# Reordering the first block of a fused SSM and GEGLU kernel: contraction outermost over seven PSUM banks, weights loaded by rows

## The chip, the cores and the metric

The kernel runs on one core of a Trainium2 chip. The metric is the device time of one execution in microseconds (us). Before the change it is 178.35 us, the median of 4 runs (178.12 to 178.73). A profile of one execution shows where the time goes; its engines are PE (TensorE, matrix products), PEld (its weight loads), DVE (VectorE), ACT (ScalarE), POOL (GpSimd) and SP (SyncE, which here only issues DMAs).

## The reference

The input x has 2048 rows (tokens) of 512 values. Everything runs on its normalized form, and three terms are added up:

```python
def _layernorm(x, axis=-1, eps=1e-5):
    m = jnp.mean(x, axis=axis, keepdims=True)
    v = jnp.var(x, axis=axis, keepdims=True)
    return (x - m) / jnp.sqrt(v + eps)

# A: a diagonal state space model, D = P = 512
    dt = jnp.exp(log_dt); Lam_bar = jnp.exp(dt * Lam)
    B_bar = ((Lam_bar - 1.0) / Lam)[:, None] * Bmat
    Bu = jnp.einsum("bld,pd->blp", x + 0j, B_bar)
    for t in range(L):
        h = Lam_bar[None, :] * h + Bu[:, t, :]
    y = 2.0 * jnp.einsum("blp,dp->bld", hseq, Cmat).real + x * Dskip[None, None, :]

# B: a gated feed-forward layer, F = 1376
    return (_gelu(x @ w_gate) * (x @ w_up)) @ w_down

    xn = _layernorm(x, axis=-1)
    return x + _A_ref(xn, ...) + _B_ref(xn, ...)
```

All inputs are bf16, and so is the output.

## The kernel before, in words

The tokens are cut into four blocks of 512 and each block into four tiles of 128. Per block the kernel normalizes (`LN`), turns the normalized tiles so that the 512 features lie on the partitions (`TR`, a transposing DMA into `XNT`), multiplies by B (`BU`), runs the scan on VectorE in a rotated frame (`CHAIN`), multiplies by w_gate and w_up and joins the two with GELU (`GU`), and sums states and hidden values into the output (`DN`). The program order of TensorE is the order of the calls at the end of `build`: the first stretch described below, `GU(0, [7, 8, 9, 10])`, `BU(0)`, `BU(1)`, `GU(1)`, `BU(2)`, `DN(0)` and so on to `DN(3)`.

Three things set the order of the rest. Operations on TensorE and DMAs on SP's queue run in the order in which they are written. Those of the other engines, DMAs on ACT's queue among them, are ordered by a planner (`Sched`): it works back from due times with assumed durations and assigns each engine its list. `order_behind` ties an operation behind another one. Semaphore waits follow from the buffers that operations read and write.

Block 0 has no weights and no x at its start, and is treated on its own. The first 896 of the 1376 columns of w_gate and w_up (seven of eleven column tiles) are computed with the tokens as rows (L684 to L711); `GU(0)` does the other four column tiles as in all later blocks. In the first stretch

- SP loads x tile by tile, w_gate and w_up in chunks of columns (`FCH`: 384, 256, 256 and the last 480), all 512 rows of a chunk at once (L505 to L514, `load_W` at L536). ACT's queue loads x's tile 1, half of the first gate chunk and the three small parameter vectors (`load_par`, L516), which a transposing DMA turns (`tr_par`, L521).
- TensorE warms up on seven 512-column products of a tile of zeros (`fwarm`, L914; `fill`, L921, repeats such products 128 columns wide).
- VectorE takes mean and variance of a tile (`stats`, L624 and L625), subtracts the mean (`sub`, L933, L941), and TensorE turns the centred tile in four 128-column transposes (`cent_T`, L673), which ACT copies from PSUM to `XC` (L680).
- `GT_mm` (L698) multiplies a centred tile by a range of columns (`FR`) of gate and up, with all four contraction steps k in succession in one PSUM bank. `GT_evac` takes GELU with the row's 1/sigma as scale on ACT (L707) and multiplies by up and 1/sigma on VectorE (L710, "hmul") into `H0`, which a DMA turns later (`H0_T`).
- POOL takes the square root of the variances (L631) after VectorE's L630; L636 is the reciprocal and L643 the full normalization, whose result `TR(0)` (L722) turns for `GU(0)` and `BU(0)`.

The order of calls in that stretch is: transposes of tiles 0 and 1; gate products of both for the first 384 columns; up products; then whole units (tile, column range), all four k at once, tiles 2 and 3 centred and turned in between.

`params` and `tables_dve` compute the scan's coefficients on POOL and VectorE from the turned parameters.

Of the kernel before, what the change touches and what calls it, by code (L numbers as in the profile page):

```python
# [77 lines left out]
class Sched:  # L78
# [95 lines left out]
    def _backward(self, span):  # L174
# [11 lines left out]
        while n:  # L186
# [26 lines left out]
            for d in op.deps:  # L213
                late[d.id] = min(late[d.id], begin[op.id] - LAT(d, op))
                left[d.id] -= 1
                if left[d.id] == 0 and d.eng not in INORDER:
                    ready[d.eng].append(d)
        return begin

    def _forward(self, prio):  # L220
# [13 lines left out]
        def rdy_time(op):  # L234
            return max([d.finish + LAT(d, op) for d in op.deps] + [op.nb])
# [55 lines left out]
    def emit(self):  # L291
# [19 lines left out]
        for e in ENGINES:  # L311
            seen = {}
            prog = []
            for op in order[e]:
                need = {}
                for d in op.deps:
                    if d.kind == "eng" and d.eng == e and (e == "tensor" or d is op.behind):
                        continue
                    key = ("e", d.eng) if d.kind == "eng" else ("d", d.id)
                    if seen.get(key, 0) >= d.val:  # L320
                        continue
                    if key not in need or need[key].val < d.val:
                        need[key] = d
# [49 lines left out]
def build(nc, ins, out):  # L373
    with ExitStack() as es:
# [16 lines left out]
        FCH = [(0, 384), (384, 640), (640, 896), (896, F)]  # L391
        WGc = [Buf("WGc%d" % i, "sbx", 10 * i, 10 * i + 1) for i in range(4)]
        WUc = [Buf("WUc%d" % i, "sbx", 100 + 10 * i, 101 + 10 * i) for i in range(4)]
# [65 lines left out]
        XCs = [[Buf("XC%d_%d" % (j, n), "xc", 2 * j + n, 2 * j + n + 1) for n in range(2)] for j in range(4)]  # L459
        H0_all = A.alloc("H0", [4, 896], BF16, at=SSb[2].lo); H0 = ring(H0_all, "H0_", 4)  # L460
        IOTJ = A.alloc("IOTJ", [512], I32, at=OUTB_all.lo)
        A1 = A.alloc("AA", [KP, 512], F32, at=TA.lo)
# [29 lines left out]
        def ld_w(W, Wc, src, ci, queue="sync", after=()):  # L492
            f0, f1 = FCH[ci]
            return S.dma(lambda e: e.dma_start(W.ap[:, :, f0:f1], src[:, f0:f1].rearrange("(k p) f -> p k f", p=128)),
                         512 * (f1 - f0) * 2, writes=[Wc[ci]], tag="ld_w", queue=queue, after=after)
# [3 lines left out]
        WG0h = [Buf("WG0h%d" % n, "sbx", n / 2, (n + 1) / 2) for n in range(2)]  # L499

        def ld_wg0(n, queue, after=()):
            return S.dma(lambda e: e.dma_start(WG.ap[:, 2 * n:2 * n + 2, 0:384],
                                        ins["B_w_gate"][256 * n:256 * (n + 1), 0:384].rearrange("(k p) f -> p k f", p=128)),
                  192 * 1024, writes=[WG0h[n]], tag="ld_w", queue=queue, after=after)
        ld_x0(0)  # L505
        S.order_behind(ld_x0(1, "scalar", [wrm]), GATE["table"])
        ld_wg0(0, "sync")
        S.order_behind(ld_wg0(1, "scalar", [wrm]), GATE["table"])
        ld_x0(2)
        ld_w(WU, WUc, ins["B_w_up"], 0)  # L510
        ld_x0(3)
        for ci in (1, 2):
            ld_w(WG, WGc, ins["B_w_gate"], ci)
            ld_w(WU, WUc, ins["B_w_up"], ci)  # L514

        def load_par():  # L516
            for q, nm in enumerate(("A_log_dt", "A_Lambda_re", "A_Lambda_im")):
                S.dma(lambda e, q=q, nm=nm: e.dma_start(PROW.ap[4 * q:4 * q + 4, :], ins[nm].rearrange("(s p) -> s p", p=128)),
                      1024, writes=[PROWq[q]], tag="ld_" + nm, queue="scalar", after=[half])

        def tr_par():  # L521
            S.dma(lambda e: e.dma_start_transpose(PAR.ap.rearrange("p q t -> p (q t)").unsqueeze(1), PROW16.ap), 4096,
                  reads=PROWq, writes=[PAR], tag="tr_par", issue=900.0)
# [12 lines left out]
        def load_W():  # L536
            ld_w(WG, WGc, ins["B_w_gate"], 3)
            ld_w(WU, WUc, ins["B_w_up"], 3)

# [8 lines left out]

        wchunk = lambda ft: 0 if ft < 3 else (1 if ft < 5 else (2 if ft < 7 else 3))
# [113 lines left out]
        def cent_T(j, banks, engs="A"):  # L663
            per = KD // len(engs)
            for n, eng in enumerate(engs):
                bank = banks[n]
                pt = PS[bank].bitcast(BF16)

                def f(e, n=n, pt=pt):
                    ins_ = None  # L670
                    for q in range(per):
                        k = per * n + q
                        ins_ = e.transpose(pt[:, 128 * q:128 * (q + 1)], XN[j].ap[:, 128 * k:128 * (k + 1)], IDN.ap)  # L673
                    return ins_
                PE(f, 56.0 * per, [XN[j], IDN], [BANK[bank]], "T0")
                dst = XC_all.ap[:, per * n:per * (n + 1), 128 * j:128 * (j + 1)]
                src = pt[:, 0:128 * per].rearrange("p (q t) -> p q t", q=per)
                w = [XCs[j][n]] if len(engs) == 2 else XCs[j]
                if eng == "A":
                    GATE["evTA"] = ACT(lambda e, src=src, dst=dst: e.activation(dst, src, ACTF.Copy), d_act(128 * per), [BANK[bank]], w, "evT")  # L680
                else:
                    V(lambda e, src=src, dst=dst: e.tensor_copy(dst, src), 110 + 0.6 * 128 * per, [BANK[bank]], w, "evT")

        FR = ((0, 192), (192, 384), (384, 640), (640, 896))  # L684

        def GT_mm(j, r, bank, us, ks=range(KD)):
            f0, f1 = FR[r]
            w = f1 - f0
            ci = max(0, r - 1)
            Wc = [(WGc, WUc)[u][ci] for u in us]  # L690
            if ci == 0 and us == [0] and len(ks) == 2:
                Wc = [WG0h[ks[0] // 2]]
            dst = PS[bank][:, w * us[0]:w * (us[-1] + 1)].rearrange("p (w f) -> p w f", w=len(us))

            def f(e):
                ins_ = None
                for k in ks:
                    ins_ = e.matmul(dst, XCd(j, k), WGU[:, us[0]:us[-1] + 1, k, f0:f1], start=(k == 0), stop=(k == KD - 1))  # L698
                return ins_
            PE(f, d_pe([w * len(us)] * len(ks)), Wc + XCs[j][ks[0] // 2:ks[-1] // 2 + 1], [BANK[bank]], "GT")  # L700

        def GT_evac(j, r, bank, rs):
            f0, f1 = FR[r]
            w = f1 - f0
            GATE["nh"] = kk = (GATE["nh"] + 1) % 3
            sc, rb = rs
            GATE["last_gelu"] = ACT(lambda e: e.activation(GG[kk].ap[:, 0:w], PS[bank][:, 0:w], ACTF.Gelu_apprx_tanh, scale=sc),  # L707
                                    d_act(w, 1), [BANK[bank], rb], [GG[kk]], "gelu")
            hp = Buf("H0_%d_%d" % (j, r), "sb", H0[j].lo + 2 * f0, H0[j].lo + 2 * f1)
            V(lambda e: e.scalar_tensor_tensor(H0[j].ap[:, f0:f1], PS[bank][:, w:2 * w], sc, GG[kk].ap[:, 0:w], ALU.mult, ALU.mult),  # L710
              d_dve_1x(w), [BANK[bank], GG[kk], rb], [hp], "hmul")  # L711
# [7 lines left out]
        def TR(b):  # L719
            tts = list(range(4 * b, 4 * b + 4))  # L720
            for j, tt in enumerate(tts):
# [64 lines left out]
        def GU_rest(b):  # L786
            k2, ft = b % 2, KF - 1
            f0, m = 128 * ft, FROWS[ft]
            for i in range(2):
# [10 lines left out]
                PE(f, d_pe([2 * m] * 8), [WGc[3], WUc[3]] + XTr(b), [BANK[bank]], "GR%d" % b)  # L800
# [11 lines left out]
        def GU(b, fts=None):  # L812
# [4 lines left out]
            def mm(ft, W, Wc, bank, c0, c1, rd):  # L817
# [8 lines left out]
                PE(f, d_pe([c1 - c0] * 4), [Wc[wchunk(ft)]] + rd, [BANK[bank]], "GU%d" % b)  # L826
# [80 lines left out]
        nwarm = 7  # L907
        wrm4 = WRM.ap.unsqueeze(1).broadcast_to([128, 4, 128])
        wb = next_bank()

        def fwarm(e, wb=wb):
            ins_ = None
            for _ in range(nwarm):
                ins_ = e.matmul(PS[wb][:, :].rearrange("p (a b) -> p a b", a=4), WRM.ap, wrm4, start=True, stop=True)  # L914
            return ins_
        PE(fwarm, d_pe([512] * nwarm) * 1.6, [WRM], [BANK[wb]], "warm")
        def fill(n):
            def f(e):
                ins_ = None
                for _ in range(n):  # L920
                    ins_ = e.matmul(PS[fb][:, 0:128], WRM.ap, WRM.ap, start=True, stop=True)  # L921
                return ins_
            PE(f, 56.0 * n, [WRM], [BANK[fb]], "fill")

        tb = [next_bank(), next_bank()]
        fb = 7
# [5 lines left out]
        def sub(j):  # L932
            return V(lambda e: e.tensor_scalar(XN[j].ap, X[j].ap, MVt[0][j].ap[:, 0:1], None, ALU.subtract),  # L933
                     d_dve_ts4x(512), [X[j], MVt[0][j]], [XN[j]], "sub")
        load_par()
        load_W()
        tr_par()
        ACT(lambda e: e.activation(H0[3].ap[:, 0:D], X[1].ap, ACTF.Copy, scale=-1.0 / D, accum_out=NM1.ap), d_act(512) + 90,
            [X[1]], [H0[3], NM1], "mean1")
        ch(*stats(0, 0)); ch(sub(0))  # L940
        ch(V(lambda e: e.tensor_scalar(XN[1].ap, X[1].ap, NM1.ap, None, ALU.add), d_dve_ts4x(512), [X[1], NM1], [XN[1]], "sub"))  # L941
        ch(*stats(0, 1))
        op, mn0, qb0, rq0 = root(0, 0, 2)
        ch(op)
        ch(*stats(0, 2)); ch(sub(2))
# [130 lines left out]
```

## Time and profile before

| | before |
|---|---|
| median of 4 runs | 178.35 us |
| profiled execution, its time | 178.56 us |
| its span, first to last instruction | 177.0 us |
| PE busy | 172.7 us, 98% |
| DVE busy | 160.7 us, 91% |
| ACT busy | 89.3 us, 50% |
| POOL busy | 10.1 us, 6% |
| DMA in the first 40th of the span / the second / the third | 165 / 315 / 318 GB/s |

A page or view of the profile names instructions by the line of the kernel's text (L698), the engine and the operation; "x20" is how many were merged into a row; "<-DMA x" behind an idle time says what ended it. Matrix products are pipelined and their ends are modelled, so one product's time in a row (379 ns for 512 columns) is longer than the distance to its successor (about 216 ns). Some 1% of the matmul records are missing from the trace (873 of 883 are there).

### The profile page before, as it was taken

What the parts mean: (1) busy time and instruction counts of PE and PEld (TensorE: products, weight loads), DVE (VectorE), ACT (ScalarE), POOL (GpSimd) and SP (SyncE); (2) the same over time, 40 slices, a digit from 0 to 9 for tenths busy, and PEclk for the clock granted to TensorE, in tenths of its full rate; (3) what the DMA queues carried; (4) which work ended last, traced back from release to release, by engine and by line L of the source; (5) the groups of instructions that cost most, each with busy time, mean ns of one, the idle gap of its engine ahead of it and who ended that gap; (6) DMA issues with size and microseconds to landing.
All of it is one profiled execution on the core that took longest, in us unless ns stands there. A gap on an engine that the chain in (4) does not pass through costs nothing.

```text
span 177.0 us, 2492 instructions
## 1 busy us (share of the span) xinstructions
PE 172.7 (98%) x873; PEld 84.9 (48%) x888; DVE 160.7 (91%) x283; ACT 89.3 (50%) x169; POOL 10.1 (6%) x25
## 2 busy tenths in 40 slices
PE   7999999999999999999999999999999999999994
PEld 2954464444644444444644444444454444444453
DVE  6969999998999979889999999899999999999821
ACT  4466678999676897003676693000667780000000
POOL 3212240200000000300000000000000000000000
PEclk9999999999999999999999999999999999999999
DMA  5996985286799300011015000100001000000311
GB/s 165 315 318 123 245 239 100 55 133 126 149 210 344 50 0 0 0 59 61 4 34 112 3 0 0 33 30 30 30 0 30 4 0 0 0 0 30 110 59 44
DMA packets 33396, 14.36 MB, mean 81 GB/s; under 512 B 23688, under 2 KB 33384, under 8 KB 33384
## 3 DMA queue, kind: packets, MB, share of 16 engines
q1 hardware_dynamic: 32944, 13.87, 32.7%
q10 hardware_dynamic: 440, 0.33, 0.7%
q8 instruction: 7, 0.11, 0.3%
q14 instruction: 5, 0.04, 0.1%
HBM read 6.46 MB, written 2.10 MB: 48 GB/s over the span
## 4 chain that ended last, share of the span: by engine, by line
PE 98%; issue 1%; DVE 0%
PE PS L864 37%; PE PS L823 32%; PE PS L734 16%; PE PS L698 7%; PE PS L797 3%; PE PS L914 2%; PE PS L673 1%; PE PS L921 0%; DVE arena L882 0%; DVE arena L479 0%; DVE arena L478 0%
## 5 line engine op out<-in xcount | busy, mean ns | idle before, releaser
L864 PE MATMUL PS<-arena 128*128 128x512 bf16 (+3 forms) x317 | 65.9, 366 | 0.3
L823 PE MATMUL PS<-arena 128*128 128x512 bf16 x258 | 57.5, 379 | 0.3
L864 PEld LDWEIGHTS PS<-arena 128*128 128x128 bf16 (+1 forms) x323 | 30.9, 98 | 35.2
L823 PEld LDWEIGHTS PS<-arena 128*128 128x128 bf16 x264 | 25.8, 98 | 30.4
L838 ACT ACTIVATE arena<-PS 128x512 bf16<-128x512 f32 x33 | 19.8, 600 | 37.5 <-PE PS L823 33.8
L767 DVE TENSOR_TENSOR_SCAN arena<-arena 128x512 bf16<-128x512 f32 x32 | 38.7, 1254 | 0.0
L734 PE MATMUL PS<-arena 128*128 128x512 bf16 x125 | 27.8, 379 | 0.2
L842 ACT ACTIVATE arena<-PS 128x512 bf16<-128x512 f32 x33 | 19.7, 597 | 5.1 <-PE PS L823 4.9
L734 PEld LDWEIGHTS PS<-arena 128*128 128x128 bf16 x128 | 12.5, 98 | 14.9
L856 ACT ACTIVATE PS<-arena 128x512 f32<-128x512 bf16 (+2 forms) x17 | 9.3, 580 | 17.5 <-DVE arena L882 17.1
L882 DVE TENSOR_TENSOR arena<-PS,arena 128x512 bf16<-128x512 f32 (+2 forms) x17 | 10.8, 652 | 7.8 <-PE PS L864 6.8
L738 ACT ACTIVATE arena<-PS 128x512 bf16<-128x512 f32 x32 | 17.2, 600 | 1.3 <-PE PS L734 1.3
L844 DVE TENSOR_TENSOR arena<-arena 128x512 bf16<-128x512 bf16 x33 | 13.1, 411 | 1.1 <-ACT arena L842 1.1
L698 PE MATMUL PS<-arena 128*128 128x192 bf16 (+2 forms) x80 | 13.4, 327 | 0.0
L624 DVE BATCH_NORM_STATS2 arena<-arena 128x6 f32<-128x512 bf16 x16 | 10.2, 680 | 0.6 <-DMA arena<-in_A_x_dram 0.6
L698 PEld LDWEIGHTS PS<-arena 128*128 128x128 bf16 x80 | 7.6, 102 | 4.8 <-issue 0.2
L756 DVE TENSOR_TENSOR arena<-arena 128x4096 bf16<-128x4096 bf16 (+1 forms) x5 | 9.2, 1857 | 0.3 <-ACT arena L620 0.3
L754 DVE TENSOR_TENSOR arena<-arena 128x4096 bf16<-128x4096 bf16 (+1 forms) x5 | 9.2, 1853 | 0.0
L779 DVE TENSOR_TENSOR arena<-arena 128x4096 bf16<-128x4096 bf16 x4 | 9.1, 2285 | 0.0
L780 DVE TENSOR_TENSOR arena<-arena 128x4096 bf16<-128x4096 bf16 x4 | 9.1, 2285 | 0.0
L707 ACT ACTIVATE arena<-PS,arena 128x192 bf16<-128x192 f32 (+1 forms) x16 | 6.5, 449 | 5.2 <-PE PS L698 5.2
L710 DVE SCALAR_TENSOR_TENSOR arena<-PS,arena 128x192 bf16<-128x192 f32 (+1 forms) x16 | 6.6, 447 | 1.9 <-ACT arena L707 1.6
(84 smaller groups left out, 110.6 us busy)
## 6 DMA issues: line engine op xcount, KB each, us to landing
out_dram<-arena SPq DMA_DIRECT2D x15, 128.0 KB, 1.7
arena<-in_A_x_dram SPq DMA_DIRECT2D x3, 512.0 KB, 4.8
arena<-in_B_w_down_dram SPq DMA_DIRECT2D x1, 1280.0 KB, 7.3
arena<-in_B_w_gate_dram SPq DMA_DIRECT2D x2, 256.0 KB, 5.1
arena<-in_B_w_up_dram SPq DMA_DIRECT2D x2, 256.0 KB, 5.5
arena<-in_B_w_gate_dram SPq DMA_DIRECT2D x1, 480.0 KB, 6.0
arena<-in_B_w_up_dram SPq DMA_DIRECT2D x1, 480.0 KB, 5.9
arena<-arena SPq DMA_TRANSPOSE x25, 2.6
```

The source lines that it names most:

```text
L624: return (V(lambda e: e.bn_stats(ST[tt].ap, X[tt].ap), d_dve_1x(512), [X[tt]], [ST[tt]], "bnst"), V(lambda e: e.bn_aggr(MVt[b][j].ap, ST[t ...
L698: ins_ = e.matmul(dst, XCd(j, k), WGU[:, us[0]:us[-1] + 1, k, f0:f1], start=(k == 0), stop=(k == KD - 1))
L734: ins_ = e.matmul(PS[bank][:, :], BBT[c][dk].ap[:, 128 * s:128 * (s + 1)], XNT[b].ap[:, dk, :], start=(dk == 0), stop=(dk == KD - 1))
L738: GATE["evBu"] = ACT(lambda e, bank=bank, k3=k3, s=s, c=c: e.activation(SSc[k3][s][c].ap, PS[bank][:, :], ACTF.Copy), d_act(512), [BANK[ba ...
L767: V(lambda e, g=g, rb=rb, init=init: e.tensor_tensor_scan(g.ap, rb, g.ap, init, ALU.mult, ALU.add), d_dve_scan(512), [g, PA[RRr]] + ([CARc ...
L823: ins_ = e.matmul(PS[bank][0:m, c0:c1], W.ap[:, dk, 128 * ft:128 * ft + m], XNT[b].ap[:, dk, c0:c1], start=(dk == 0), stop=(dk == KD - 1))
L838: GATE["last_gelu"] = ACT(lambda e, bg=bg, kk=kk, m=m: e.activation(GG[kk].ap[0:m, :], PS[bg][0:m, :], ACTF.Gelu_apprx_tanh), d_act(512), ...
L842: ACT(lambda e, bu=bu, kk=kk, m=m: e.activation(UPB[kk].ap[0:m, :], PS[bu][0:m, :], ACTF.Copy), d_act(512), [BANK[bu]], [UPB[kk]], "evU")
L844: V(lambda e, kk=kk, m=m, ft=ft, k2=k2: e.tensor_tensor(HTt[k2][ft].ap[0:m, :], GG[kk].ap[0:m, :], UPB[kk].ap[0:m, :], ALU.mult), d_dve_tt ...
L856: ACT(lambda e: e.activation(PS[bank][:, c0:c1], X[tt].ap[:, c0:c1], ACTF.Copy), d_act(c1 - c0), [X[tt]], [BANK[bank]], "seed")
L864: ins_ = e.matmul(PS[bank][:, c0:c1], l_[:, 128 * j:128 * (j + 1)], r_[:, c0:c1], start=False, stop=last and n == len(ops) - 1, skip_group ...
L882: V(lambda e: e.tensor_tensor(OUTB[ko].ap[:, c0:c1], PS[bank][:, c0:c1], XD[tt].ap[:, c0:c1], ALU.add), d_dve_1x(c1 - c0), [BANK[bank], XD ...
```

## The change

The first stretch of block 0 is rewritten; from `params` on the calls are the same.

- **Loads.** The first 896 columns of w_gate and w_up come as rows: for each k, 128 rows of gate, then 128 rows of up (`ld_wk`), the remaining 480 columns later (`ld_w`). ACT's queue loads x's tiles 1 and 2. The parameter vectors are loaded behind the copies of the transposes, and are turned on TensorE (`tr_par`) and copied by ACT.
- **Tiles 0 and 1.** Tile 0's mean is a tensor_reduce on VectorE, without a variance; the first 128 columns of a tile are centred by themselves and turned by one transpose, the other 384 columns by three more. `GT_k` makes one contraction step for one tile and column range, into one of seven PSUM banks that stay open (`acc`); k is the outermost loop over both tiles, gate and up and four ranges (256, 256, 256, 128 columns).
- **Tiles 2 and 3** are normalized in full, turned by the transposing DMA (`TR(0, [2])`, `TR(0, [3])`) and multiplied from `XNT` (`GT_mm`), with no scale in the evacuation. Tile 3's variance is a Square on ACT.
- **Warm-up** multiplies a constant tile of ones, which the program has before its first instruction.
- **The planner** learns that an operation ordered behind a DMA waits for its issue, not for its landing.

```diff
-                late[d.id] = min(late[d.id], begin[op.id] - LAT(d, op))
+                late[d.id] = min(late[d.id], begin[op.id] + d.dur - d.issue if d is op.behind and d.kind == "dma" else begin[op.id] - LAT(d, op))
...
+        def ld_wk(W, Wc, src, k):
+            return S.dma(lambda e: e.dma_start(W.ap[:, k, 0:FS], src[128 * k:128 * (k + 1), 0:FS]),
+                         256 * FS, writes=[Wc[k]], tag="ld_w")
...
         ld_x0(0)
         S.order_behind(ld_x0(1, "scalar", [wrm]), GATE["table"])
-        ld_wg0(0, "sync")
-        S.order_behind(ld_wg0(1, "scalar", [wrm]), GATE["table"])
-        ld_x0(2)
-        ld_w(WU, WUc, ins["B_w_up"], 0)
-        ld_x0(3)
-        for ci in (1, 2):
-            ld_w(WG, WGc, ins["B_w_gate"], ci)
-            ld_w(WU, WUc, ins["B_w_up"], ci)
+        S.order_behind(ld_x0(2, "scalar", [wrm]), GATE["table"])
+        for k in range(KD):
+            if k == 2:
+                ld_x0(3)
+            ld_wk(WG, WGc, ins["B_w_gate"], k)
+            ld_wk(WU, WUc, ins["B_w_up"], k)
...
+        def acc(j, u):
+            return (3, 256 * j) if u == 3 else (4 * j + u, 0)
+
+        def GT_k(k, j, u, ws, first=False):
+            f0, f1 = FR[u]
+            w = f1 - f0
+            bank, c0 = acc(j, u)
+            dst = PS[bank][:, c0 + w * ws[0]:c0 + w * (ws[-1] + 1)].rearrange("p (w f) -> p w f", w=len(ws))
+            PE(lambda e: e.matmul(dst, XCd(j, k), WGU[:, ws[0]:ws[-1] + 1, k, f0:f1], start=first, stop=k == KD - 1, skip_group_check=True), ...)
...
+        mean(1, NM1)
+        ch(V(lambda e: e.tensor_reduce(SUM0.ap, X[0].ap, mybir.AxisListType.X, ALU.add), 600, [X[0]], [SUM0], "sum0"))
+        ch(cent(0, 0), cent(0, 1))
+        fill(2)
+        ch(cent_T(0, 0, 1, 7, "V"))
+        ch(cent(1, 0), cent(1, 1))
+        fill(4)
+        GT_k(0, 0, 0, [0], True)
+        cent_T(1, 0, 1, 6, "A")
+        for u in (1, 2, 3):
+            GT_k(0, 0, u, [0], True)
+        cent_T(0, 1, 4, 7, "A")
+        cent_T(1, 1, 4, 5, "A")
+        par_ld = load_par()
+        for u in range(4):
+            GT_k(0, 0, u, [1])
+        for us in ((0, 3, 2), (1,)):
+            for w_ in range(2):
+                for u in us:
+                    GT_k(0, 1, u, [w_], w_ == 0 and u < 3)
...
+        ch(recip(qb(2, 3), rq(2, 3)), norm(2))
+        TR(0, [2])
+        ld_w(WG, WGc, ins["B_w_gate"])
...
+        ch(recip(qb(0, 2), rq(0, 2)), norm(0), norm(1))
+        ch(recip(qb(3, 4), rq(3, 4)), norm(3))
+        TR(0, [3])
+        ld_w(WU, WUc, ins["B_w_up"])
+        TR(0, [0, 1])
+        ld_x(1)
+        for k in (1, 2):
+            for w_ in range(2):
+                for j in range(2):
+                    for u in range(4):
+                        GT_k(k, j, u, [w_])
+        tr_par(7)
+        for j, u in ((0, 0), (0, 1), (0, 2), (1, 0), (1, 1), (1, 2), (0, 3), (1, 3)):
+            GT_k(3, j, u, [0, 1])
+            if u < 3:
+                bank, c0 = acc(j, u)
+                GT_evac(j, u, bank, (RQ.ap[:, 0, j:j + 1], rq(j, j + 1)), c0)
...
+        for (j, u), bank in zip([(j, u) for j in (2, 3) for u in range(4)], (7, 0, 1, 2, 4, 5, 6, 3)):
+            GT_mm(j, u, bank)
+            GT_evac(j, u, bank, None)
```

In the program as built, VectorE's first list is: reduce, cent(0), copy of the first transpose, cent(1), statistics of tile 2, of tile 0, reciprocal and normalize 2, statistics of tile 1, reciprocal and normalize 0 and 1, a product that reads the turned parameters, reciprocal and normalize 3, then the hmuls. SP's first list is: x tile 0, the rows of k = 0 and 1, x tile 3, the rows of k = 2 and 3, TR(2), w_gate's tail, TR(3), w_up's tail, TR(0), TR(1), x of block 1, B.

## The prediction

> **What bounds the kernel now.** I read the busy shares first, then the chain that ended last, then the waits, and last the windows and DMA issues of the first 20 us, where the change lies.
>
> ```profile
> PE 172.7 (98%) x873; PEld 84.9 (48%) x888; DVE 160.7 (91%) x283; ACT 89.3 (50%) x169; POOL 10.1 (6%) x25
> ```
>
> ```profile
> 1.02 3.17 PE PS L914 x7
> 4.19 0.21 PE PS L921 x2
> 4.40 0.93 PE PS L673 x8
> 5.33 1.36 PE PS L698 x8
> 6.69 0.22 PE PS L921 x4
> 6.92 0.99 PE PS L698 x12
> ...
> 10.67 8.21 PE PS L698 x40
> 18.88 0.05 issue
> 18.93 5.13 PE PS L823 x23
> ```
>
> The chain (start, length, what) is TensorE from end to end. The waits name one for it, the warm-up's own start, and from 4.30 on matmuls start back to back (the 0.05 "issue" pieces are missing records). So block 0's end is a sum of columns, and what matters is when the first matmul of GU(0) starts. Ends are modelled 0.16 us late and one record is missing before 18.93: GU(0) starts at 18.72. The same chain shows the clock: 0.43 us per 512 columns at L914 and 0.170 per 192 in the first eight L698, 0.083 in the next twelve. It doubles at about 6.57 us.
>
> ```profile
> PE PS L914 <- DVE arena L479: 1.0, 1, 1.0
> ```
>
> ```profile
> 3.50:7.00 3.50, 3.50 (x27) 2.75 (x26) 3.25 (x12) 1.73 (x5) 0.90 (x2) 1.00 0.99 292
> 7.00:10.50 3.50, 3.50 (x40) 2.91 (x38) 3.26 (x11) 1.84 (x5) 0.89 (x2) 1.00 1.13 345
> ```
>
> In the windows (last two columns: DMA share, GB/s) the DMA engines are full from 3.5 to 14 us: 292 to 345 GB/s, which is the pace at which weights can come.
>
> **The change part by part.** Times are us of the profiled execution, 178.56 (span 177.0 and 1.5 around it); the median of the four runs is 178.35, 0.21 lower.
>
> *TensorE columns.* GATE/UP work is 4 tiles x 4 k x 1792 = 28,672 columns before and after. PE transposes fall from 16 to 8 (tiles 2 and 3 now come through the transposing DMA), 1,024 columns = 8 x 0.056 = 0.45 us at the fast clock. Added: tr_par on PE, 0.03, and 8 more matmuls by 2.5 ns, 0.02.
>
> *Start.* Before: statistics 0.69 + 0.18 and sub 0.35 behind x landing at 2.92, first transpose at 4.30.
>
> ```profile
> L624 DVE BATCH_NORM_STATS2 arena<-arena 128x6 f32<-128x512 bf16 x4 | 2.8, 688 | 0.6 <-DMA arena<-in_A_x_dram 0.6
> L933 DVE TENSOR_SCALAR arena<-arena 128x512 bf16<-128x512 bf16 x3 | 1.1, 355 | 0.1
> L710 DVE SCALAR_TENSOR_TENSOR arena<-PS,arena 128x192 bf16<-128x192 f32 x8 | 2.9, 410 | 0.1
> ```
>
> After: one tensor_reduce, which the trace lacks; between a 512-wide TENSOR_SCALAR (0.355) and a statistics pass (0.688) I take 0.69, since it too reads 512 elements into one number. Then the 128-wide cent: 0.164 (a two-element operation, L630) to 0.355, by width 0.21. With 0.05 per handover the first transpose starts at 2.94 + 0.69 + 0.06 + 0.21 + 0.05 = 3.95. The warm-up no longer waits for a memset (1.02 becomes about 0.75, when ACT and SP start), so it and fill(2) end at 0.75 + 2.99 + 0.21 = 3.95 and do not delay it. VectorE's copy of that transpose from PSUM stands behind the 384-wide cent (0.30): bounds 0.164 and 0.410, taken 0.33. First real matmul at 4.63; fill(4) ends at 4.50, so it costs nothing. The shorter sub-chain is worth little: if the reduce took 0.35 the gain would be 0.1, since fill(4) then sets the start.
>
> [...]
>
> *The sum.* From 4.63 to 6.57 the slow clock does 1.94 x 1200 = 2,330 columns. Work from there is 28,672 + 7 transposes x 128 + 16 = 29,584; the remaining 27,254 take 11.36 at 2.4 GHz, 81 matmuls by 2.5 ns 0.20. GU(0) starts at 6.57 + 11.56 = 18.13 against 18.72: 0.59 earlier. As a check: transposes -0.45, fill(4) now wholly in the slow stretch -0.19 (before, most of it ran after 6.57), small additions +0.05.
>
> *What must hide.* (a) Row loads. X and the 896-column rows are 2,304 KB, as many as the first eleven loads before, the last of which (L494 issued at 4.78) took 5.7 to land, 10.5. TensorE reaches k=1 at 7.5, k=2 at 9.0 and k=3 at 10.6, and wants the w_up half 0.75 later in the first two; at the old pace (landings of the trace) the bytes through both rows of k=1, 2 and 3 are there at 7.2, 9.1 and 10.5, and 128 descriptors of 1,792 B per load instead of 512 of 512 to 768 should not be slower. Cost 0; if the last row comes 0.3 late, 0.2. Before, other weights covered such a delay; with the contraction outermost nothing else is left to do.
> (b) The parameter loads move on ACT's queue from 1.92 to behind the last PE-transpose copy, about 6.2; the last issues at 7.1. tr_par waits for them on TensorE in front of all k=3 work. Bounds for landing: X's 2.2 and the weights' 6.0 us, so 9.3 to 13.1 against 10.5. The nearest rows are loads on that queue, 2.3 and 3.8 (the trace's semaphore times give the three small ones 3.3, 2.8 and 3.3, behind a weight load). I take 2.8, 9.9: no wait.
> (c) Queue of SP. Its order is now TR(2), w_gate tail, TR(3), w_up tail, TR(0), TR(1), ld_x(1). TR(2)'s normalize ends at 7.5; it lands behind the rows at about 11.2, TensorE wants it at 12.1. Tile 3's normalize stands on VectorE behind a product that reads the parameters (tr_par at 10.6, ACT copy, then product, reciprocal, normalize 0.41): 11.6. TR(3) issues for 1.27 and lands at 14.2, wanted at 15.2. Then w_up's tail 0.5, TR(0) 1.3, TR(1) issued at 14.8.
>
> ```profile
> L722 SPq DMA_TRANSPOSE arena<-arena x4: 1188/1259/1265, 9.5 to 13.7; - x4
> ...
> DMA to landing us min/median/max: 2.6/3.5/4.4
> ```
>
> TR(1) lands at 17.4 to 19.2; I take 17.4, since those with 3.5 and more had 960 KB or more ahead and this has 480. GU(0) wants it at 18.13.
> (d) Banks: hmul by 0.48 each starts at 11.7; bank 0 is wanted at 12.9 and every later one has more room. Cost 0. mean and sq3 of tile 3 sit on ACT, idle half the time; VectorE loses 4 subs (1.4) and one statistics pass (0.87) and gains the reduce, four cents and a copy (about 2.0), so its end of block 0 stays within 0.3.
> (e) After block 0 the program is the same but for the planner's orders. The 0.59 passes only where cover is left: BU(1) starts at 32.30 and its last transpose, issued at 28.48, lands at 31.0, 1.3 spare; x(1) is issued about 1 us later but VectorE uses it at 21.0 and it lands near 20.3. The last scan block ends at 161.3 for matmuls at 162.8, 1.5 spare. So it passes.
>
> 178.56 - 0.59 = 177.97; on the median, 178.35 - 0.59 = 177.76, **177.8**.
>
> **The clock.** Both kernels pay for the late doubling; it moves little between them if it stays at 6.57. [...] The trace shows only the one instant.
>
> **The rivals.** 0.3% is 0.54 us, about what a measurement of this kernel tells from none.
> - *Given back in front of k=3* (rows or parameters 0.3 to 0.9 late). For: the old pace lands the last row at 10.5, exactly when wanted, and TensorE has no other work. Against: longer descriptors, an empty ACT queue. Price: gain 0 to 0.35, 178.0 to 178.4, no change.
> - *The last transposes decide, slower.* TR(1) stands behind a chain of PE, ACT, VectorE and five SP issues. If w_up's tail issues in 1.4 as one load did at 5.89, TR(1) is issued at 15.7, and with 3.5 to 4.4 to landing GU(0) starts at 19.2 to 20.1: 0.5 to 1.4 later than now, 178.8 to 179.7. It costs the gain beyond 18.72 and shows as slower beyond 19.25. Against: the ring is no longer backed up by then.
> - *The clock doubles earlier*, as the warm-up starts 0.27 earlier. The 2,330 columns at the slow clock cost 0.97 more than at the fast one, which is all that can come; the rows, at 345 GB/s there by about 9.8, leave some 0.7 of it. Gain 0.7 to 1.3, 177.1 to 177.6.
> - *It does not do what it says*: another engine order later eats it. VectorE is 91% busy; cover is 1.3 us, so this needs a new stall of that size. Counted in the first rival.
>
> **How the numbers follow.** Forecast 0.50 (its own range 177.4 to 178.2: reduce and copy at their bounds -0.1/+0.05, waits to 0.3, the median's 0.2); given back 0.23; last transposes 0.21; clock 0.06. The forecast splits 0.43 faster, 0.07 within 0.3%; the second rival 0.19 slower, 0.02 within; the clock is faster. Faster 0.49, same 0.32, slower 0.19. The range runs from 177.1 to 178.9: it holds the clock case and the lower end of the slow one, leaving out some 0.15.
>
> **What would show it.** Right: seven matmuls from about 0.75; first transpose near 3.95; TensorE without a gap from 4.6; GU(0) at 18.1 to 18.2; everything after shifted alike. Wrong: a gap in front of the one-row transpose or of k=2 or k=3 (late loads), a gap in front of the tile-2, tile-3 or GU(0) matmuls with the transposing DMA as releaser, or a gap at BU(1). A doubling of the clock at another time than 6.6 us would move both terms.

## The result, and the profile after

The changed kernel is slower. Its median is 179.67 us (178.42 to 182.84, 17 executions) against 178.28 us (177.91 to 178.77, 27 executions) of the kernel before; the ratio is 1.0072, 95% interval 1.0058 to 1.0085. The forecast was 177.8 in 177.1 to 178.9. Medians in this text are over all executions of a run; the ratios leave out single disturbed ones.

The first profile misleads: it is of an execution of 178.65, one of the few short ones; 13 of the 17 took 179.5 to 180.2. Its busy shares are nearly those of before:

```profile
PE 172.8 (98%) x874; PEld 85.2 (48%) x889; DVE 160.0 (90%) x285; ACT 89.0 (50%) x172; POOL 12.1 (7%) x26
```

The chain that ended last, first 20 us (start, length, what):

```profile
0.77 3.14 PE PS L924 x7
3.92 0.21 PE PS L932 x2
4.13 0.11 PE PS L663
4.24 0.43 PE PS L932 x4
4.66 0.35 PE PS L685
...
6.30 4.43 PE PS L685 x44
10.72 0.09 issue
10.81 0.16 PE PS L522
10.97 1.64 PE PS L685 x8
12.61 5.63 PE PS L696 x28
```

The warm-up starts at 0.77 and the first real matmul at 4.64, as forecast. The gap at 10.72 is new: the one-row transpose `tr_par` (L522) waits for the parameters. GU(0) (L832) is recorded at 18.80 with 23 of its 24 products; the missing one is the first, so it starts at 18.58, against 18.72 before. Of the 0.59 expected, 0.14 is there. (All 32 products of L696 are in the trace; the chain shows 28, since from 18.24 on it names an operation on ACT, L709, which ends at 18.74, as what released the record at 18.80. The missing first product started before that.)

The operations that the prediction had to price, by form (the last numbers are count, busy us and mean ns), and the DMA-bound stretches (last two columns: DMA share, GB/s):

```profile
L954 DVE TENSOR_REDUCE arena<-arena 128x1 f32<-128x512 bf16 x1 | 0.7, 687 | 0.6 <-DMA arena<-in_A_x_dram 0.6
L944 DVE TENSOR_SCALAR arena<-arena 128x128 bf16<-128x128 bf16 x1 | 0.3, 256 | 0.0
L673 DVE TENSOR_SCALAR arena<-PS 128x128 bf16<-128x128 bf16 x1 | 0.2, 225 | 0.2 <-PE PS L663 0.2
```

```profile
3.50:7.00 3.50, 3.50 (x27) 2.71 (x25) 2.49 (x10) 1.57 (x5) 0.20 (x1) 1.00 0.96 268
7.00:10.50 3.50, 3.50 (x38) 3.19 (x36) 2.48 (x10) 1.53 (x4) 1.81 (x5) 1.00 0.86 294
```

TensorE is without a gap in both stretches although the DMA engines moved less than before (268 and 294 against 292 and 345 GB/s): the rows of weights did not hold it up here.

GU(0) stands behind the transposing DMAs of tiles 0 and 1, issued at 13.9 and 15.1. The view of their line, L731, restricted to these two, has in its last line the time from issue to landing:

```profile
DMA to landing us min/median/max: 3.3/3.6/4.0
```

Tile 1's landed at 18.38, and GU(0) started 0.20 later. The rest of the small gain is gone behind it: at BU(1) block 1's last transposing DMA lands at 31.94 (30.99 before), TensorE waits 0.2 (its products there start 0.42 apart instead of 0.22), and it ends at 174.56 against 174.50.

### The profile page after: what moved, and what is told of

Its sections match the earlier page's. It is cut to its first block, busy times and chain, and to the rows that moved or that the text cites. A ratio compares the mean times of both kernels' runs of the same rounds, so it can differ in the third digit from the quotient of the medians.

```text
span 176.8 us, 2504 instructions
## 1 busy us (share of the span) xinstructions
PE 172.8 (98%) x874; PEld 85.2 (48%) x889; DVE 160.0 (90%) x285; ACT 89.0 (50%) x172; POOL 12.1 (7%) x26
## 4 chain that ended last, share of the span: by engine, by line
PE 94%; ACT 4%; issue 1%; DVE 0%; ACTq 0%
PE PS L873 37%; PE PS L832 32%; PE PS L743 12%; PE PS L685 4%; PE PS L696 3%; PE PS L806 3%; PE PS L924 2%; ACT arena L747 1%; ACT arena L613 1%; ACT arena L614 1%; PE PS L663 0%; PE PS L932 0%; ACT arena L709 0%; DVE arena L891 0%; PE PS L522 0%
## 5 line engine op out<-in xcount | busy, mean ns | idle before, releaser
L832 PE MATMUL PS<-arena 128*128 128x512 bf16 x258 | 57.5, 379 | 0.4
L832 PEld LDWEIGHTS PS<-arena 128*128 128x128 bf16 x264 | 25.7, 98 | 30.4 <-issue 0.2
L743 PE MATMUL PS<-arena 128*128 128x512 bf16 x125 | 28.0, 379 | 0.2
L743 PEld LDWEIGHTS PS<-arena 128*128 128x128 bf16 x128 | 12.5, 98 | 15.1 <-issue 0.5
L747 ACT ACTIVATE arena<-PS 128x512 bf16<-128x512 f32 x32 | 17.4, 597 | 0.7 <-PE PS L743 0.6
L618 DVE BATCH_NORM_STATS2 arena<-arena 128x6 f32<-128x512 bf16 x15 | 9.5, 680 | 0.9 <-DMA arena<-in_A_x_dram 0.9
L685 PE MATMUL PS<-arena 128*128 128x256 bf16 (+2 forms) x56 | 7.3, 287 | 0.0
L696 PE MATMUL PS<-arena 128*128 128x512 bf16 (+1 forms) x32 | 6.2, 352 | 0.0
L598 DVE SCALAR_TENSOR_TENSOR arena<-arena 128x512 bf16<-128x512 bf16 x8 | 5.5, 743 | 0.8 <-ACT arena L595 0.8
L685 PEld LDWEIGHTS PS<-arena 128*128 128x128 bf16 x56 | 5.2, 103 | 1.5 <-issue 0.2
```

Of the source, the lines that this page charges most:

```text
L618: return (V(lambda e: e.bn_stats(ST[tt].ap, X[tt].ap), d_dve_1x(512), [X[tt]], [ST[tt]], "bnst"), V(lambda e: e.bn_aggr(MVt[b][j].ap, ST[t ...
L685: PE(lambda e: e.matmul(dst, XCd(j, k), WGU[:, ws[0]:ws[-1] + 1, k, f0:f1], start=first, stop=k == KD - 1, skip_group_check=True), d_pe([w ...
L696: ins_ = e.matmul(dst, XNT[0].ap[:, k, 128 * j:128 * (j + 1)], WGU[:, :, k, f0:f1], start=(k == 0), stop=(k == KD - 1))
L743: ins_ = e.matmul(PS[bank][:, :], BBT[c][dk].ap[:, 128 * s:128 * (s + 1)], XNT[b].ap[:, dk, :], start=(dk == 0), stop=(dk == KD - 1))
L747: GATE["evBu"] = ACT(lambda e, bank=bank, k3=k3, s=s, c=c: e.activation(SSc[k3][s][c].ap, PS[bank][:, :], ACTF.Copy), d_act(512), [BANK[ba ...
L832: ins_ = e.matmul(PS[bank][0:m, c0:c1], W.ap[:, dk, 128 * ft:128 * ft + m], XNT[b].ap[:, dk, c0:c1], start=(dk == 0), stop=(dk == KD - 1))
```

## The experiments

**The changed kernel again (r1).** No edit; the question is what a typical execution looks like.

> The changed kernel, unchanged, to get a second profile. Its one profile so far is of an execution of 178.65, in the lower tail of its times: TensorE lost 0.25 in front of the one-row transpose (parameters at 10.68) and 0.30 in front of GU(0) (18.80, tile 1's transposing DMA at 18.38). Most executions take 179.5 to 180.1, about 1.2 more. T1 (the last transposes decide): GU(0) at 19.7 to 20.2, released by the transposing DMA, TensorE without new gaps before. T2 (the parameters are late): a gap of 1.2 to 1.7 in front of the one-row transpose, at 10.7. [...] T4 (block 1's transposes): GU(0) at 18.8 and a gap of 1.2 in front of BU(1).

Median 179.89 against 178.13, ratio 1.0096 (1.0080 to 1.0112). The profile is of an execution of 179.63. What TensorE waited for (total, times, longest):

```profile
PE PS L832 <- DVE arena L566: 1.5, 1, 1.5
PE PS L924 <- PEq L1109: 0.8, 1, 0.8
PE PS L522 <- DMA arena<-in_A_Lambda_im_dram: 0.5, 1, 0.5
PE PS L685 <- DVE arena L673: 0.2, 1, 0.2
```

GU(0) starts at 19.80. The releaser in the first line is only the event that came last before it: in the first profile the same VectorE instruction runs after GU(0) has started. The same view of L731 for the transposing DMAs of tiles 0 and 1, here issued at 13.5 and 14.7, tells what it waited for:

```profile
DMA to landing us min/median/max: 4.9/5.3/5.7
```

Tile 1's landed at 19.61, 0.19 in front of GU(0). It was issued 0.4 earlier than in the first profile and took 4.89 instead of 3.26. T1, then. The clock is not the cause: it doubled at 3.84 in this execution, 2.8 earlier than in the first profile, and the execution was still 1.0 longer.

What the DMA engines did from 16.75 to 19.25, in 40 slices (busy share in tenths, GB/s, then each queue's packets, MB and share), first in the short execution, then in this one:

```profile
DMA  9999999999999969464746999955799899999999
GB/s 305 264 257 254 222 176 258 271 291 287 291 279 299 152 127 210 115 189 131 164 115 213 213 147 213 147 147 180 246 295 262 295 344 344 393 344 410 360 426 344
...
q1 hardware_dynamic: 1359, 0.62, 105.8%
```

```profile
DMA  9979999999999999000000010010100000799999
GB/s 217 447 160 222 263 266 266 262 283 262 234 111 49 49 37 16 0 0 0 0 0 4 8 8 8 8 12 8 12 8 8 12 8 12 185 393 360 344 426 328
...
q1 hardware_dynamic: 893, 0.31, 130.8%
q8 instruction: 1, 0.02, 3.1%
```

In the second, a packet of the instruction queue (q8, 16 KB) starts at 16.86. A view counts a packet's bytes where it starts: from 17.7 to 18.8 all 16 engines together start 0 to 16 GB/s, and 22 packets of 4 to 1024 bytes that started just before last 1.2 to 1.5 us (0.01 to 0.05 is the usual time). In the first execution that packet started at 21.68, behind everything that GU(0) needs. This is the reason formed here (theory H below): the packet holds the transposing DMAs beside it. The kernel before has the same packet at 14.48; the same view of it for 14.25 to 16.75:

```profile
GB/s 0 0 0 262 0 0 0 0 0 0 70 152 217 205 201 225 197 205 197 172 74 42 4 4 8 8 8 8 12 8 8 12 8 8 12 8 25 0 0 0
...
q8 instruction: 1, 0.02, 3.2%
```

The same plateau of 4 to 12 GB/s, 15.6 to 16.5. Tile 3's transposing DMA runs beside it (issued 13.72, landed 17.20, 3.48 against 2.64 for the one issued before it) and still has 1.5 to spare.

**Parts undone: early parameters (r2), tile 0 first (r3), the old warm-up (r4).**

```diff
 # r2
-            last = GATE["evTA"]
+            last = x0_2                  # behind x tile 2 on ScalarE's queue
 # r3
+        TR(0, [0])
         TR(0, [3])
         ld_w(WU, WUc, ins["B_w_up"])
-        TR(0, [0, 1])
+        TR(0, [1])
 # r4
-        ones = nc.const_aps.tensor(1.0, (128, 128), BF16)
+        ones = WRM.ap                    # zeros, waits for its memset
```

> The three parameter loads go out on ScalarE's queue straight behind the x tiles, as before the change, and land at about 6 instead of 10.5. T2: the time falls to about 178.4, 1.2 below the changed kernel. T1: 0 to 0.3 below it, as tile 3's normalization still sets the queue. [...]

> The transposing DMA of tile 0 goes in front of tile 3's, into the time in which SP's queue waits for tile 3's normalization; tile 1's is then issued about 1.2 earlier. T1: the wait in front of GU(0) goes, 178.3 to 178.6, 1.0 to 1.3 below the changed kernel. [...] T4: some of the gain, as all later DMAs of the queue go out 1.2 earlier.

> The warm-up multiplies the tile of zeros again, as before the change, and so waits for its memset; everything else is that of the changed kernel. It starts at about 1.0 instead of 0.77, and the first transpose is at about 4.2. [...] T1, T2, T4: 0 to 0.3 above the changed kernel.

Ratios: r2 1.0082 (1.0051 to 1.0113), r3 1.0063 (1.0036 to 1.0090), r4 1.0073 (1.0044 to 1.0101). None restores the time, so neither the late parameters (T2) nor the new warm-up are the cause alone. In r4's profile the clock doubles at 6.6 to 6.8, as in the first profile (6.60, an execution of 178.65), and the median is 179.52. r3, at 179.24, misses the 178.3 to 178.6 that T1 gave it. What TensorE waited for shows why; first a line of r2's profile, then r3's:

```profile
PE PS L698 <- DMA arena<-arena: 1.2, 1, 1.2
```

```profile
PE PS L743 <- DMA arena<-arena: 1.6, 1, 1.6
PE PS L924 <- PEq L1110: 0.8, 1, 0.8
PE PS L522 <- DMA arena<-in_A_Lambda_im_dram: 0.2, 1, 0.2
```

In r2 the wait for the parameters is gone, but the packet came at 13.91, and tile 3's transposing DMA (issued 12.06) landed at 16.02: TensorE waits in tile 3 (L698). In r3 tile 1's lands at 18.04 and GU(0) starts at 18.33 without a wait; but BU(1) (L743) waits 1.6 for block 1's transposing DMAs. The packet (17.59) now runs beside block 1's x, which lands at 21.25 instead of 20.44. That explains little: in r8 (below) it lands at 21.25 as well. The difference is on SP's queue; the first two of block 1's transposing DMAs, in r3 and in r8 (times of issuing in ns):

```profile
L731 SPq DMA_TRANSPOSE arena<-arena x2: 1196/2042/2888, 25.3 to 26.6; - x2
```

```profile
L731 SPq DMA_TRANSPOSE arena<-arena x2: 1189/1192/1195, 24.9 to 26.2; - x2
```

In r3 the second one takes 2.89 to issue instead of 1.19, so the third goes out at 29.48 instead of 27.63, though VectorE has had its tile ready since 27.0. A packet of another instruction queue (q14, 8 KB) runs from 27.24 to 29.15; whether it held the issue is open, since r9 and r10 have one of 2.05 and 1.75 without such an issue. In r4 the packet comes at 17.17 and tile 1's takes 4.73: GU(0) at 20.11.

**The packet moved (r5, r6, r8).** A packet of q8 comes about every 255 TensorE records (240 to 268 in the two profiles of the changed kernel), so the count of instructions was changed and the work left alone.

```diff
 # r5: 42 records more, same columns
-            for _ in range(nwarm):
-                ins_ = e.matmul(PS[wb][:, :], ones, ones4, start=True, stop=True)
+            for _ in range(4 * nwarm):
+                ins_ = e.matmul(PS[wb][:, 0:128], ones, ones, start=True, stop=True)
 # r6: about 110 more; fill likewise
+            for _ in range(8 * nwarm):
+                ins_ = e.matmul(PS[wb][0:32, 0:64], ones[:, 0:32], ones[:, 0:64], start=True, stop=True)
 # r8: 32 fewer, at k = 1 and 2
-                        GT_k(k, j, u, [w_])
+                    GT_k(k, j, u, [0, 1])
```

> The seven 512-column products of the warm-up become 28 of 128 columns: the same columns, 42 more TensorE records (products and weight loads). Theory H: a 16 KB packet of the instruction queue, which brings TensorE its next instructions about every 257 records, runs beside the last transposing DMAs of block 0 and holds them for about 1.4; the first one is due at about 150 records, 10.8 to 11.4 in the changed kernel, and started between 13.9 and 21.7. With 42 records more it is due at about 8.5 and should start by 13, in front of tile 1's transposes: tile 1 then lands at 18.4, GU(0) starts at 18.1 to 18.8 and the time is 178.3 to 178.8, 0.9 to 1.4 below the changed kernel. Rival P (the place in the queue, behind w_up's tail, is all there is): GU(0) stays at 19.8 to 20.1 and the time at 179.6, whatever the packet does.

> The warm-up and fillers become 56 and 12 products of 64 columns by 32: some 110 TensorE records more, about the same time. Theory H: the first packet is due at about 5, so it is over by 11 at the latest, and the second one comes at 22 to 30 instead of 34 to 36. Tile 1 lands at 18.4 and GU(0) starts at 18.1 to 18.8; where the second packet then meets block 1's transposing DMAs (25 to 32), BU(1) waits instead. 178.3 to 178.8 without that, up to 1.5 more with it. Rival P: GU(0) at 19.8 to 20.1, time 179.6.

> For k = 1 and 2 one 512-column product takes the two of 256 columns for gate and up: 32 TensorE records fewer, the same columns. The packet is due 32 records later, at about 14. Theory H: it starts at 16.9 or later, in some executions only behind tile 1's transposes; the time is 179.6 as long as it comes at 17 and 178.5 where it comes later. Rival P: 179.6 in every execution.

Ratios: r5 1.0058 (1.0032 to 1.0085), r6 1.0120 (1.0093 to 1.0146), r8 1.0054 (1.0034 to 1.0075).

r6 is the clean case. The packet starts at 8.70, and the plateau follows it; the DMA view of r6 for 8.5 to 11.0:

```profile
GB/s 373 250 185 381 115 86 29 29 98 172 221 217 217 233 201 217 160 135 70 25 8 8 8 8 12 8 12 8 8 12 8 13 0 0 46 31 77 92 123 108
...
q8 instruction: 1, 0.02, 2.3%
```

It holds the last row of weights (landed 10.50), which has the time. The transposing DMAs of tiles 0 and 1, in the same place on the queue as in the changed kernel, land by the view of L731 within

```profile
DMA to landing us min/median/max: 3.3/3.7/4.1
```

as in the short execution, and GU(0) starts at 18.93. So the place in the queue (rival P) is not enough; what differs is where the packet runs. But the next one moved as well, to 28.22 from 34 to 36, among block 1's transposing DMAs (packets up to 3.1 long), and TensorE waits there, by the waits of r6:

```profile
PE PS L743 <- DMA arena<-arena: 1.0, 1, 1.0
```

This run is slower than the changed kernel: its median is 180.66, 0.4 above the most that H allowed (180.3); the profile is of its shortest execution, 179.89. r5 missed: its median, 179.58, is the figure of P. Its profile is of its longest execution, 181.30: TensorE waits 0.7 for the first row of w_gate there, the clock doubles at 9.0, the packet starts at 18.67 and tile 1's takes 4.75. In r8 the packet came at 17.23 and tile 1's took 4.78; its times (179.2 to 179.8) are what both H and P expected, so r8 does not tell them apart.

Six profiles with this order of DMAs, from the trace (where the first product of GU(0) is not recorded, in r5, r6, r8 and the first profile, its start is taken 0.216 ahead of the second's):

| run | packet starts | tile 1's DMA issued, landed | took | GU(0) starts |
|---|---|---|---|---|
| r6 | 8.70 | 15.39, 18.73 | 3.34 | 18.93 |
| first profile | 21.68 | 15.12, 18.38 | 3.26 | 18.58 |
| r1 | 16.86 | 14.72, 19.61 | 4.89 | 19.80 |
| r4 | 17.17 | 15.18, 19.91 | 4.73 | 20.11 |
| r8 | 17.23 | 14.98, 19.76 | 4.78 | 19.96 |
| r5 | 18.67 | 16.50, 21.25 | 4.75 | 21.44 |

Where the packet runs between the issue and the landing, the DMA takes 1.4 to 1.6 more, and in all six GU(0) starts 0.19 to 0.20 behind the landing. r2 has this order as well: there the packet was over (13.91 to 14.91) when tile 1's was issued at 16.04, and it took 2.55.

**Room for the DMAs (r7, r9 to r11).** If a hold can't be kept away, what it falls on must have time. r7 changes only SP's order. In r9 GU(0) also does its three gate tiles first, so that w_up's tail is wanted 1.7 later; r10 adds the early parameters, turned before k = 2, and puts tile 3's normalization ahead of the first hmul; r11 adds the merged products of r8.

```diff
 # r7
-        TR(0, [3])
-        ld_w(WU, WUc, ins["B_w_up"])
-        TR(0, [0, 1])
+        TR(0, [0]); TR(0, [3]); TR(0, [1])
+        ld_w(WU, WUc, ins["B_w_up"])
 # r9: as r7, but ld_x(1) in front of ld_w(WU), and in GU for block 0
+                for i, ft in enumerate(fts[:3]):
+                    banks[ft] = (bk[i], bk[3 + i])
+                    mm(ft, WG, WGc, bk[i], 0, 512, XTr(b))
```

> On SP's queue the transposing DMAs of tiles 0, 3 and 1 all go in front of w_up's tail. Rival P: tile 1 lands at about 16.5 and w_up's tail at about 17.9 to 18.5, both before they are wanted (18.1 and 19.0), so GU(0) starts at 18.1 to 18.4; what is left is BU(1). Theory H: tile 1 lands early as well, and the packet holds w_up's tail or x of block 1 instead: a wait of up to 1.0 inside GU(0)'s first products of w_up, or, as in the run with tile 0 first, a wait of 1 to 2 in front of BU(1). 178.4 to 179.6 by H, 178.3 by P.

> GU(0) multiplies its three gate tiles first and its three up tiles behind them, so that w_up's tail is wanted at about 20.7 instead of 19.0; on SP's queue the transposing DMAs of tiles 0, 3 and 1 and x of block 1 go in front of w_up's tail. The parameters stay late. Theory H (the instruction packet holds whatever DMA runs at its time for about 1.4, and what decides is the spare time of that DMA): tile 1 lands at 16 to 17.5 even when held, x of block 1 at 17.5 to 19.5, w_up's tail by 20.4; GU(0) starts right behind tile 3, at 17.5 to 18.6 by the clock and the 0.3 to 0.7 of wait for the parameters; no wait of over 0.3 in front of BU(1). 178.0 to 178.7. If the earlier chain (TensorE's own start, the parameters) were what costs the time, it stays at 179.3 to 179.7.

> As the run before, and the parameters are loaded early, turned on TensorE between k = 1 and k = 2, and tile 3's normalization stands in front of the first product of the evacuation on VectorE. Theory H: also the waits of 0.3 to 0.7 at the one-row transpose go; tile 3's transposing DMA is issued at about 11.3 instead of 12.0 and lands at 13.7 to 15.2. GU(0) at 17.1 to 18.2; 177.4 to 178.1, 0.3 to 0.9 below the kernel before. If the packet falls on tile 3's transposing DMA (it was held to 16.0 in the run with early parameters), up to 0.8 more.

> As the run before, with one 512-column product for gate and up also at k = 1 and 2: 32 TensorE records fewer, so that the instruction packet is due at about 14 instead of 11 and falls behind tile 3's transposing DMA. Theory H: 177.4 to 178.1 as there, without the part that a held tile 3 can cost; the held DMA is x of block 1 or w_up's tail, which have the time. If it falls on tile 1's, which is wanted at 17.1 to 18.2: up to 0.5 more.

Ratios: r7 1.0054 (1.0033 to 1.0076), r9 1.0053 (1.0032 to 1.0075), r10 1.0008 (0.9985 to 1.0030), r11 1.0006 (0.9994 to 1.0018). r7 (179.30) is where H put it and not at P's 178.3, but not for H's reason alone: GU(0) starts without a wait at 19.06, since the parameters cost 0.7, and BU(1) waits 0.8, again behind an issue of 2.94 beside a packet of q14. r9, r10 and r11 (179.37, 178.63, 178.43) missed their ranges; r9's time lies in the range that its expectation gave for an earlier chain as the cause. In its profile tile 1's lands at 16.32, GU(0) starts at 18.60, and waits elsewhere add up; from the waits:

```profile
PE PS L685 <- DMA arena<-in_B_w_up_dram: 0.9, 1, 0.9
...
PE PS L879 <- DVE arena L792: 0.7, 1, 0.7
PE PS L743 <- ACT arena L747: 0.2, 1, 0.2
```

The first is k = 0's row of w_up, landed at 6.55, with the clock doubled at 4.9; the second is a scan block wanted by DN(1), at 110, and is more than half of what r9 loses on the kernel before. Why it comes late there was not followed. From r9 to r10 the time falls by 0.7: with room for the DMAs the early parameters and the order on VectorE are worth something that r2 did not show; the two were not separated. r10's profile is of an execution of 177.86 and names no wait of TensorE behind the warm-up: GU(0) starts at 18.02, 0.7 ahead of the kernel before, and TensorE ends 0.7 ahead of it. So a gain of the forecast's size is there in an execution without waits; but r10's executions go from 177.8 to 179.8, and one to 181.2. r11's are closer together, 178.0 to 179.0.

**Block 1's transposing DMAs freed (r12, r13).** In r11 the last of them still lands at 31.91, and TensorE waits 0.36 in front of BU(1), by the distance of its products.

```diff
 # in load_B
-            ld_x(2)
 # in build
         TR(1)
+        ld_x(2)
```

> The run gates first, merged, with the load of block 2's x (512 KB) on SP's queue behind block 1's four transposing DMAs instead of in front of them. If these transposes take the gain back: they land at 30.5 or earlier instead of 31.9 and the wait of 0.36 in front of BU(1) goes; 177.6 to 178.1, 0.3 to 0.8 below the kernel before. If block 0's own end is the bound (rows behind an early clock): 178.2 to 178.5, as without this edit.

> The same load order with the 256-column products at k = 1 and 2 (gates first, not merged), whose times spread from 177.8 to 179.8. If block 1's transposes make that spread: 177.5 to 178.0 with a spread under 0.8. If the instruction packet on block 0's transposes makes it: the spread stays, and the median is 178.3 to 178.6.

r12: median 178.19 against 178.39, ratio 0.9988 (0.9971 to 1.0005). r13: 178.28, 0.9992 (0.9975 to 1.0008). Block 1's four transposing DMAs land sooner; the view of their line from 24 to 29, first in the changed kernel's first profile, then in r12's:

```profile
DMA to landing us min/median/max: 3.2/4.5/5.2
```

```profile
DMA to landing us min/median/max: 2.5/2.8/3.8
```

The last one lands at 30.94 and BU(1) no longer waits, but the time lies between the two expectations and is no clear gain on the kernel before. In r12's profile (clock doubled by 4.7) TensorE waits for k = 0's and k = 1's rows of w_up, 0.3 and 0.4, and GU(0) starts at 18.13. r13's spread stayed (177.5 to 179.1), so block 1's DMAs alone did not make it. In r13's profile (178.75) TensorE waits 0.6 for a row of w_up and 0.5 for w_up's tail, which landed at 21.44 after 6.2; in r10 to r12 it took 4.7 to 5.0. r12 is the best version here: by the ratios some 1.5 us below the changed kernel, and level with the kernel before.

## Why the prediction was wrong

*TensorE's start: right.* First transpose 3.93 (forecast 3.95), first matmul 4.64 (4.63), reduce 0.687 (0.69), first cent 0.256 (0.21), copy from PSUM 0.225 (0.33). The rates in the forecast's sum are those of the profile before: 0.0825 us per 192 columns (0.99 for 12) and 0.2158 per 512 (L823 from 39.19: 5.18 for 24) give 2.4 columns per ns and about 2.5 ns per matmul, and 0.43 per 512 in the warm-up half that rate. The columns were right too: 18.13, plus 0.04 for start and clock, 0.25 and 0.10 at the one-row transpose and 0.08 of wait for tile 1's DMA, is 18.60; the first profile has 18.58.

*(a) Rows: right at a late clock, wrong at an early one.* With the clock at 6.6 (first profile) the rows of k = 1 to 3 were there 0.67 or more before use. With the clock at 3.8 to 4.9 (r9, r11, r12, r13) TensorE waited 0.3 to 0.9 for rows of w_up; in r1, at 3.84, it waited 0.2 at L685, by its waits for VectorE's copy (L673). That the longer descriptors should be no slower was the author's estimate and was not shown: from 3.5 to 7 and from 7 to 10.5 the DMA engines moved 268 and 294 GB/s, against 292 and 345 before.

*(b) Parameters: mis-sized.* Forecast to land at 9.9 with no wait; they landed at 10.0 to 11.2 in the profiles with late loads, and cost 0.25 (first profile), 0.6 (r1) and up to 0.7 (r7). `tr_par` itself cost 0.13 with its handover, not 0.03. This is the first rival's place, and it is real; r2 shows that taking it away alone does not bring the time back, and r10 that it counts once the DMAs have room.

*(c) Queue of SP: the step that failed, with (e) behind it.* Tile 1's transposing DMA was issued at 15.1 (forecast 14.8), but "I take 17.4, since those with 3.5 and more had 960 KB or more ahead and this has 480" read the row of before wrongly. Of the four DMAs in that row the last took 3.48 with nothing large ahead: w_up's tail had landed at 13.23, before it was issued. It is the one beside the instruction packet; its neighbour, landed before the packet's plateau, took 2.64. So bytes ahead do not sort that row, and 2.6 to landing was no safe value. In the changed kernel tile 1's took 3.3 without the packet beside it and 4.7 to 4.9 with it. It landed at 18.38 at best and at 19.6 to 19.9 in the three profiles of executions of 179.6 to 180.0 (r1, r4, r8), not at 17.4, and GU(0) started at 19.8 to 20.1, not at 18.13. That the packet is what holds the DMA rests on these profiles and on r6, in which the packet was moved away; the hold as such has one profile per edit behind it.

*(e) "So it passes": wrong by what was left of the cover.* BU(1) had 1.1 to spare before, not 1.3: its first product starts at 32.12, and the prediction's 32.30 is read from the chain, in which the modelled ends shift the starts. In the changed kernel block 1's last transposing DMA comes 0.95 later and BU(1) earlier, so there is none left: 0.2 of wait in the first profile, 0.8 to 1.6 in r3, r6 and r7. Had GU(0) come 0.59 earlier, this alone would have taken the gain: with the landing at 31.94 BU(1) starts at 32.19, whenever GU(0) is done. The first profile shows it, without the packet beside tile 1's DMA: 178.65 against 178.56. In r12 that DMA lands at 30.94, GU(0) starts at 18.13, and the profiled execution takes 177.98.

*The rivals.* "The last transposes decide, slower" happened: GU(0) at 19.8 to 20.1 stands within its 19.2 to 20.1, and 179.67 in its 178.8 to 179.7. Its place was right; its mechanism was not the one. It named an issue at 15.7 and 3.5 to 4.4 to landing, and the issue came at 14.7 to 15.2 with 4.7 to 4.9 to landing (w_up's tail issued in 0.59 in the first profile, not in 1.4), so that its numbers fit is in part luck. "The clock doubles earlier" happened too, by more than was thought: the profiles of these runs show 3.8 to 6.6, and 9.0 in r5. That the earlier warm-up brings it is not shown: with its start at 1.02 the clock doubled at 6.57 before, with 0.77 at 6.60 in the first profile. The early clock brings nothing here: r1 had the clock at 3.84 and was longer than the first profile with 6.60, since the DMA set GU(0).

*What stays open.* Why the packet starts where it does: 13.9 to 21.7 in the profiles with the changed kernel's instruction count, 3 to 10 after the count at which it seems due. Why the issue of a transposing DMA takes 2.9 in r3 and r7. And why the runs with room for the DMAs (r10 to r13) are not 0.6 faster in the median, as single executions of them are: that early clocks only run into the rows is argued from four profiles, not shown.

## What to carry to other kernels

Read a DMA's issue-to-landing time together with the instruction queues: if a packet of theirs runs beside it, its time is not its own (here 4.7 to 4.9 us instead of 3.3), and a row's spread must not be explained by bytes alone. In this kernel a packet cost a transposing DMA 1.4 to 1.6 us, so what TensorE needs next wants about that much time ahead of use wherever such a packet can fall, as the kernel before had for its last transposing DMA; and when an early stage is shortened, check that the stage behind it keeps its cover. Where executions of one kernel scatter more than those of its neighbour, one profile is not the kernel: take a second before explaining.

## What the runs showed of the hardware

- In eight of the fifteen profiles the DMA engines, with DMAs not yet landed, start only 5 to 9 GB/s together for 0.9 to 1.4 us, beginning 0.5 to 1.2 us after the start of the first 16 KB instruction packet (0.9 to 1.8 long itself). In r3, r13 and r9 there are 18 to 20 packets of 256 bytes that last 0.9 to 1.8 (0.02 is usual) instead, beginning 1.7, 2.8 and 3.7 after it; whether they belong to it is not shown. The first profile, r2 and r7 have stops of 0.4 to 0.6 only; in r10 nothing stands out. In r10 a packet of the other instruction queue (q14, 8 KB, at 19.75) is followed by such a plateau from 20.4 to 20.9. The transposing DMA beside the 16 KB packet took 1.4 to 1.6 longer (4.73 to 4.89 in r1, r4, r5 and r8, 3.26 and 3.34 in the first profile and r6). That these packets bring TensorE its instructions is the author's reading of the queue's name and of the 240 to 268 records between them; no run shows it. What in the engines makes the hold was not tried.
- In the eight profiles of the changed kernel and its variants that record it, all with a warm-up from 0.77 on, the TensorE clock doubled at 3.80, 3.84, 4.42, 4.92, 5.88, 5.90 and 6.60 us after the span's start, and at 8.96 in r5, where TensorE had stood still for 0.7 at 5.3.
